# A state-space scan and a two-layer perceptron in one kernel: eleven transfers for a unit's loads instead of twenty, and another order of the head

## The chip, the cores and the metric

One NeuronCore of a Trainium2 chip. The metric is the device time of one execution in microseconds, the median of several runs. The engines are PE (TensorE), DVE (VectorE), ACT (ScalarE), POOL (GpSimd) and SP (SyncE), which here does nothing but issue transfers. [...]

## The reference

Two blocks in a row, all in float32. The first is a Mamba-2 scan (4 sequences, 8 heads, 768 steps, head dimension 32, state dimension 16), given in chunks:

```python
for c in range(nc):
    cum = np.cumsum(log_a[chunk c], axis=-1)
    L = np.exp(cum[i] - cum[j]) * causal
    y_intra = (C @ B.T * L) @ x
    y_inter = (C @ state) * np.exp(cum)
    state = np.exp(sum(log_a)) * state + sum over j of (B[j] x[j] exp(cum[-1] - cum[j]))
```

Its output, as 3072 tokens of 256 features, goes through `h = x @ w_in` (256 to 2048), `g = h * sigmoid(h)` and `g @ w_out` (2048 to 256).

## The kernel before, in words

**Units and pairs.** The 3072 tokens are 12 units of 256 tokens, three to a sequence; a unit has four chunks of Q = 64. The scan of a unit feeds half of the 512 token columns of a pair of units, and the perceptron works pair by pair. Pair 0 (units 0 and 1) uses plain float32 products (`f_s1`, L491, and `f_s2`, L504); pairs 1 to 5 use three products of split numbers (`fp32r`): h, l and d parts of the weights (`WH`, `WL`, `WD`, made by `w_h`, `w_l`, `w_d`, L197 to L209) and of the tokens (`XH`, `XL`, `XD`, made by `f_xh`, `f_xl`, `f_xd`).

**One unit's scan.** DVE's transposes `f_T` (L352), or PE's `f_TP` (L360) for units 1 and 2, give B and C by state. `f_P` scans the decays over each chunk (`pfx`, L311, from `pz`), and `f_C` makes `cw`. `scan_E` (L324) makes the decay matrix E from `ab`, which holds each chunk's decays broadcast over 64 rows, in two halves; `f_B` makes BT from E. Then on PE `f_G` (L402) and `f_D0` (L390), on DVE `f_S` (L422, states) and `f_M` (L408, E times G), on ACT `f_SM`, on PE `f_Y` (L442, L451), and on ACT `f_X`, which copies out the unit's tokens.

**Loads.** `load_unit` (L139) issues everything of a unit on SP's queue: `pz` (4 transfers), B and C by rows (`tbc`, 4 each), B by tokens (`bn`, 2), `ab` (4) and x (2): twenty. Unit 2 has C by tokens in place of the `tbc` loads, so fourteen. `pz` and `ab` come from two DRAM copies of the clipped decays, `a_in` and `a_zero`, which `f_A2` writes in the head. Units 0 and 1 get theirs from the inputs directly.

**Weights.** Sixteen weight pieces of 512 KB arrive as 64-bit numbers (`raw`, six buffers in the pool `quad`); ACT (`w_size`), DVE and POOL (`w_bits`, L181) turn each into float32 (`w32`). `w_bits(n)` then issues the load of piece n + 6, so the place of a `w_bits` in the program also fixes the place of a load in SP's queue. Pieces 0 to 7 are of `w_in`, 8 to 15 of `w_out`.

**Order.** The kernel is under a manual schedule: every engine's order is the order of the calls. The head (L624 to L680) is written out call by call. Then `steps` (L732) lists which `f_s1(u, j)` follows which and what is put between: "2:D b9 s10" is `f_G` and `f_D0` of unit 2, `w_bits(9)`, `w_size(10)`. A second list (L738) does the same around `f_s2(0)` to `f_s2(5)`, written m0 to m5; h, l and d with a number are `w_h`, `w_l`, `w_d`, and `3:h`, `3:l`, `3:d` are `f_xh`, `f_xl`, `f_xd` of unit 3. After that `step(s)` (L755) runs the f32r pairs: `s1_d` (L515) starts a tile's sum and sends it through ACT (L520), `s1_h` (L522) goes on, `s2` and `s2_d` are the second layer. `PLAN` puts the units of the next pair between the steps ("bL" is the load of the second unit after).

**Pools.** `quad` has six buffers of 4 KB a partition, `blk` 76 of 2 KB. `loads` gives `ab`, `tbc` and `bn` one buffer each, `xt` two.

Of the kernel before, what the change touches and what calls it, by code (L numbers as in the profile page):

```python
# [8 lines left out]
FP32 = mybir.dt.float32  # L9
# [24 lines left out]
def kernel(  # L34
# [22 lines left out]
    nc = tc.nc  # L57

    batch, H, S, D = x.shape
    N = B.shape[-1]  # L60
    Q = 64
    UT = 256
# [6 lines left out]

    const = ctx.enter_context(tc.tile_pool(name="const", bufs=1))  # L70
    loads = ctx.enter_context(tc.tile_pool(name="loads", bufs=1))
    quad = ctx.enter_context(tc.tile_pool(name="quad", bufs=6))
    sc = ctx.enter_context(tc.tile_pool(name="sc", bufs=1))
    sc2 = ctx.enter_context(tc.tile_pool(name="sc2", bufs=2))
    blk = ctx.enter_context(tc.tile_pool(name="blk", bufs=1))
    dram = ctx.enter_context(tc.tile_pool(name="dram", bufs=1, space=bass.MemoryType.DRAM))
    ps_s = ctx.enter_context(tc.tile_pool(name="ps_s", bufs=1, space=bass.MemoryType.PSUM))
    ps_h = ctx.enter_context(tc.tile_pool(name="ps_h", bufs=2, space=bass.MemoryType.PSUM))
# [19 lines left out]
    ab, bn, tbc, xt = ({} for _ in range(4))  # L98
# [2 lines left out]
        return u // UPB, u % UPB * UT  # L101

    def load_pa(u, q):
        for c in range(4):
            q.dma_start(out=pz[:, c, 1:], in_=a_in[4 * u + c].rearrange("h (o t) -> h o t", o=1).to_broadcast([H, N, Q]))

    def load_ab(u, q):
        ab[u] = loads.tile([128, 2, H, Q], FP32, name="ab")
        for t in range(4):
            k, c = divmod(t, 2)  # L110
            q.dma_start(out=ab[u][64 * c:64 * c + 64, k], in_=a_zero[4 * u + t:4 * u + t + 1].to_broadcast([64, H, Q]))

    def load_n(u, i, q):
        b, t0 = at(u)
# [8 lines left out]
    def load_t(u, i, q):  # L123
        b, t0 = at(u)
        if u == 0:
            tbc[u] = block("tbc0").rearrange("p (i e r n) -> p i e r n", i=2, e=2, r=8)
        elif u not in tbc:
            tbc[u] = loads.tile([128, 2, 2, 8, N], FP32, name="tbc")
        for g in range(4):
            q.dma_start(out=tbc[u][32 * g:32 * g + 32, i],  # L130
                        in_=(B, C)[i][b, 2 * g:2 * g + 2, t0:t0 + UT].rearrange("e (t r) n -> t e r n", r=8))

    def load_x(u, q):
        b, t0 = at(u)
# [46 lines left out]
    def w_bits(n, parts=1):  # L181
        if n in raw:
            u, v, hi = two(wu.pop(n)), two(wv.pop(n)).bitcast(U32), raw[n][:, :, :, 1]
            nc.vector.tensor_scalar(out=u, in0=u, scalar1=LEAST, scalar2=MOST, op0=ALU.max, op1=ALU.min)
            u = u.bitcast(U32)
            nc.vector.tensor_scalar(out=u, in0=u, scalar1=3, scalar2=None, op0=ALU.logical_shift_left)
            nc.vector.scalar_tensor_tensor(out=v, in0=hi, scalar=0x80000000, in1=v,  # L187
                                           op0=ALU.bitwise_and, op1=ALU.bitwise_or)
            w32[n] = block("w32")
            for i in range(parts):  # L190
                fs = slice(WF // parts * i, WF // parts * (i + 1))
                nc.gpsimd.tensor_tensor(out=two(w32[n])[:, :, fs].bitcast(U32), in0=u[:, :, fs], in1=v[:, :, fs],  # L192
                                        op=ALU.add)
        if n + RAW < NW:
            load_w(n + RAW, nc.sync)
# [13 lines left out]
                                       op0=ALU.mult, op1=ALU.subtract)  # L209


    a_in = dram.tile([batch * S // Q, H, Q], FP32, name="a_in")
    a_zero = dram.tile([batch * S // Q, H, Q], FP32, name="a_zero")
    NC0 = S // Q
    A0, A1 = 96, 96 + NC0
# [30 lines left out]
    def f_A2():  # L246

        r = slice(0, NC0 * batch)
        nc.vector.tensor_scalar(out=acl[r], in0=acl[r], scalar1=1.0, scalar2=1e-6, op0=ALU.min, op1=ALU.max)
        nc.vector.tensor_copy(out=acz[r], in_=acl[r])  # L250
        nc.vector.memset(acz[r, :, 0:1], 0.0)
        nc.sync.dma_start(out=a_in, in_=acl[r])
        nc.sync.dma_start(out=a_zero, in_=acz[r])

    misc = block("misc")
    idle = misc[:, 0:UT].bitcast(BF16)
    nc.vector.memset(idle, 0.0)

    def busy(n, small=0):
        t = half("zero")  # L260
# [55 lines left out]
    def f_P(u):  # L316
        if u < 2:
            f_P0(u)
        f_P1(u)
# [15 lines left out]
    def f_Ek(u, k):  # L335
        scan_E(u, H * k, H, ab.pop((u, k)))
# [8 lines left out]
    def f_B(u, engine=nc.vector):  # L345
        BT[u] = sc.tile([128, 2, H, N], FP32, name="BT")
        engine.tensor_tensor(out=BT[u], in0=bn[u], in1=E[u][:, :, :, Q - 1:Q].to_broadcast([128, 2, H, N]),
                             op=ALU.mult)
# [138 lines left out]
    def f_s1(u, j):  # L487
        hp = two(half("hp"))
        for i in range(2):
            for kc in range(KC):  # L490
                nc.tensor.matmul(out=hp[:, i], lhsT=two(w32[j])[:, kc, 128 * i:128 * i + 128],  # L491
                                 rhs=two(XF[u])[:, kc], start=(kc == 0), stop=(kc == KC - 1))
        GT[u, j] = block("gT")
        nc.scalar.activation(two(GT[u, j]), hp, AF.Silu)
        if j == 7:
            XF.pop(u)
# [17 lines left out]
    def s1_d(s):  # L514
        P, f = 1 + s // NF, s % NF  # L515
        HP[s] = half("hp")
        for kc in range(KC):
            nc.tensor.matmul(out=HP[s], lhsT=two(WD[f // 2])[:, kc, 128 * (f % 2):128 * (f % 2) + 128], rhs=XD[P][:, kc],  # L518
                             start=(kc == 0), stop=False, skip_group_check=True)
        nc.scalar.activation(HP[s], HP[s], AF.Copy, scale=-HALF / UP)  # L520
# [125 lines left out]
    w_size(1)  # L646
    busy(3, 18)
    f_Y(0)
    f_P(1)
    f_Ek(1, 0)  # L650
    f_Ab(1, 1)
    f_X(0)
# [5 lines left out]
        f_T2(1, e)  # L658
    f_s1(0, 1)
    f_Ek(1, 1)  # L660
    f_B(1)
    w_bits(2, 2)
    f_C(1)
# [5 lines left out]
    f_M(1, 0)  # L669
    f_M(1, 1)  # L670
    f_s1(0, 2)
    f_A2()
    load_unit(2)
    w_size(4, "u")
    w_bits(3, 2)
    f_Y(1)
    f_X(1)
    w_size(4, "v")
# [43 lines left out]
    def todo(text):  # L722

        for step in text.split():
            if ":" in step:
                u, what = step.split(":")
                stage(int(u), what)
                continue
            n = int(step[1:].split(".")[0])
            {"b": w_bits, "s": w_size, "h": w_h, "l": w_l, "d": w_d, "m": f_s2, "o": f_out0}[step[0]](n)  # L730

    steps = ((1, 0, ""), (0, 3, "b5 s6"), (1, 1, "b6 s7"), (1, 2, "b7 s8"), (1, 3, "b8"), (0, 4, "2:T"),  # L732
             (1, 4, "2:P"), (0, 5, "2:C12B s9 3:L"), (1, 5, "2:D b9 s10"), (0, 6, "2:SsM"), (1, 6, "b10 s11"),
             (0, 7, "2:Y b11 s12 3:T"), (1, 7, "b12 s13 3:P h0"))
    for u, j, text in steps:
        f_s1(u, j)
        todo(text)
    for text in ("m0 3:C12B 2:h h1 l0 d0 2:l b13 s14", "m1 3:D 2:d 4:L h2 l1 d1 b14 s15", "m2 3:SsM h3 l2 d2 b15",  # L738
                 "m3 3:Y h4 l3 d3", "m4 3:h h5 l4 d4 h8 3:l", "m5 3:d l5 d5 4:T l8 d8"):
        todo(text)  # L740


# [12 lines left out]
    def step(s):  # L755

        last = NF * (NP - 1)
        t = s - LAG
        P, f = 1 + s // NF, s % NF
        ends = t >= 0 and t % NF == NF - 1  # L760
        scans = P + 1 < NP
        if t >= 0:
            PENDING.append(t)
        if s == 0:
            s1_d(0)

        if s < last:
            s1_h(s)
            if s + 1 < last:
                s1_d(s + 1)  # L770
        if scans and f in FIRST:
            stage(2 * P + 2 + "ab".index(FIRST[f][0]), FIRST[f][1:])
        if s == last + 1:
            s2(t)
            s2_d([t, t + 1])
            f_sum2(NP - 1)
            return
        if s == last + 2:
            s2(t)
            f_end(NP - 1)  # L780
            return
        if ends:
            s2_d(PENDING)
            s2(t)
            PENDING.clear()
            f_out(1 + t // NF)
        if s < last:
            s1_g(s)
        if s < 2:
            f_s2(6 + s)  # L790
        if s == 2:
            f_out0(0)
            f_out0(1)
        if t >= 0 and not ends:
            s2(t)
        if PENDING and not (scans and (f < 6 or 9 <= f < 12)):
            s2_d(PENDING)
            PENDING.clear()
        if scans and f == 8:
            f_sum2(P)  # L800
        if 1 <= s <= last:
            s1_gl(s - 1, nc.gpsimd if f in ASIDE and scans else nc.vector)
            s1_gd(s - 1)
        if s >= last:
            return
        if t > 4 and t % NF == 2:
            f_store()
        if scans:
            for what in PLAN.get(f, ()):
                u = 2 * P + 2 + "ab".index(what[0])  # L810
                if f == 15 or what == "aL":
                    u += 2
                if u < NU:
                    stage(u, what[1:])
        if s in PARTS:
            w_h(PARTS[s])
        if s - 1 in PARTS:
            w_l(PARTS[s - 1])
            w_d(PARTS[s - 1])
# [34 lines left out]
```

## Time and profile before

| | before |
|---|---|
| time, median of 3 runs | 349.65 us (349.64 to 349.75) |
| span of the profiled execution | 346.5 us, 7826 instructions |
| PE busy | 324.6 us, 94% |
| DVE busy | 262.6 us, 76% |
| ACT busy | 211.9 us, 61% |
| POOL busy | 66.1 us, 19% |
| DMA | 26.66 MB in 99339 packets |

A busy share is a mean over the whole span. Which engine sets the pace of a stage is seen in the busy times by stretch, in the gaps that an engine's timeline shows, and in the chain of waits, which follows the work that ended last back to what released it. "SPq" is time in which SP issues a transfer. "DMA raw<-..." in a chain is the wait for such a transfer to land.

### The profile page before, as it was taken

The numbers are of one execution on the slowest core, as the hardware profiler recorded it, in microseconds if no ns is written. First come the engines' busy times: TensorE is split into PE (matmuls) and PEld (weight loads), VectorE is DVE, ScalarE is ACT, GpSimd is POOL, SyncE is SP. The second block draws the span as 40 slices with busy tenths as digits, with TensorE's granted clock in tenths as the row PEclk, the third lists the DMA queues.
The fourth block names the chain that finished last, engine by engine and source line by source line (L and its number), as shares of the span: only waits on it lengthen the run. The fifth ranks groups of instructions, "written<-read, shape, count | busy, mean of one in ns | idle before, by whom it ended". The sixth has DMA issues, their size and how long they took to land.

```text
span 346.5 us, 7826 instructions
## 1 busy us (share of the span) xinstructions
PE 324.6 (94%) x3145; PEld 254.3 (73%) x3146; DVE 262.6 (76%) x430; ACT 211.9 (61%) x403; POOL 66.1 (19%) x56
## 2 busy tenths in 40 slices
PE   8977999777998999999999999999999999999991
PEld 4566788666866778777778778778778788788881
DVE  7969975999559998898766896965996853674443
ACT  3656575432467877757775756666676756555651
POOL 3235523120113010242101231202250202000000
PEclk9999999999999999999999999999999999999998
DMA  6975894650171160045340163420153000020003
GB/s 121 209 248 173 168 335 98 145 115 0 48 144 25 38 117 1 18 108 83 67 97 0 34 120 67 88 63 1 48 112 57 2 2 0 0 48 14 0 0 63
DMA packets 99339, 26.66 MB, mean 77 GB/s; under 512 B 87558, under 2 KB 92422, under 8 KB 99302
## 3 DMA queue, kind: packets, MB, share of 16 engines
q1 hardware_dynamic: 95110, 25.76, 33.1%
q10 hardware_dynamic: 4192, 0.39, 0.9%
q8 instruction: 24, 0.39, 0.5%
q14 instruction: 13, 0.11, 0.1%
HBM read 22.80 MB, written 3.34 MB: 75 GB/s over the span
## 4 chain that ended last, share of the span: by engine, by line
PE 70%; DVE 10%; DMA 8%; SPq 8%; issue 2%; ACT 1%; DVEq 0%; ACTq 0%
PE hp L526 22%; PE b L572 11%; PE hp L518 10%; PE oa L559 10%; PE oa L558 10%; DMA raw<-in_moe_w_out_dram 3%; SPq L121 3%; PE oa L504 2%; DVE wl L203 2%; PE gy L451 2%; DMA ab<-a_zero 2%; PE gy L442 1%; DMA a_in<-acl 1%; DMA raw<-in_moe_w_in_dram 1%; PE gy L402 1%
## 5 line engine op out<-in xcount | busy, mean ns | idle before, releaser
L520 ACT ACTIVATE hp<-hp 128x512 f32<-128x512 f32 x80 | 46.6, 582 | 75.0 <-PE hp L518 74.7
L540 DVE TENSOR_TENSOR gl<-g,gh 128x512 fp32r<-128x512 f32 x56 | 38.6, 689 | 47.7 <-ACT gh L536 44.8
L540 POOL TENSOR_TENSOR gl<-g,gh 128x512 fp32r<-128x512 f32 x24 | 39.9, 1663 | 172.4 <-ACT gh L536 156.3
L526 PE MATMUL hp<-xh,wh 128*128 128x512 f32 x160 | 65.6, 410 | 2.6 <-ACT hp L520 2.6
L544 DVE SCALAR_TENSOR_TENSOR gd<-gh,g 128x512 fp32r<-128x512 f32 x80 | 61.9, 776 | 6.0 <-ACT gh L536 6.0
L526 PE MATMUL hp<-xl,wl 128*128 128x512 f32 x160 | 63.2, 395 | 0.0
L559 PE MATMUL oa<-gl,wl 128*128 128x512 f32 x160 | 63.1, 394 | 0.0
L558 PE MATMUL oa<-gh,wh 128*128 128x512 f32 x160 | 62.7, 392 | 0.0
L536 ACT ACTIVATE gh<-g 128x512 fp32r<-128x512 f32 x80 | 50.6, 632 | 2.8
L518 PE MATMUL hp<-xd,wd 128*128 128x512 f32 x160 | 50.4, 396 | 0.0
L534 ACT ACTIVATE g<-hp 128x512 f32<-128x512 f32 x80 | 47.5, 594 | 0.6 <-PE hp L526 0.6
L572 PE MATMUL b<-gd,wd 128*128 128x512 f32 x160 | 44.6, 391 | 0.0
L526 PEld LDWEIGHTS hp<-xh,wh 128*128 128x128 f32 x160 | 30.0, 188 | 13.0 <-ACT hp L520 6.0
L558 PEld LDWEIGHTS oa<-gh,wh 128*128 128x128 f32 x160 | 30.0, 188 | 7.5 <-ACT o L584 0.7
L518 PEld LDWEIGHTS hp<-xd,wd 128*128 128x128 f32 x160 | 30.0, 188 | 7.3
L559 PEld LDWEIGHTS oa<-gl,wl 128*128 128x128 f32 x160 | 30.0, 188 | 7.2
L572 PEld LDWEIGHTS b<-gd,wd 128*128 128x128 f32 x160 | 30.0, 188 | 6.8 <-DVE o L599 0.2
L526 PEld LDWEIGHTS hp<-xl,wl 128*128 128x128 f32 x160 | 30.1, 188 | 5.5
L491 PE MATMUL hp<-xf,w 128*128 128x256 f32 x128 | 30.1, 386 | 4.3 <-POOL w L192 3.0
L192 POOL TENSOR_TENSOR w<-wu,wv 128x512 uint32<-128x512 uint32 (+1 forms) x20 | 23.4, 1178 | 50.5 <-DVE wv L187 47.8
L491 PEld LDWEIGHTS hp<-xf,w 128*128 128x128 f32 x128 | 23.5, 190 | 9.7 <-POOL w L192 4.5
L324 DVE TENSOR_TENSOR_SCAN E<-ab,diag 128x512 f32<-128x512 f32 x24 | 28.7, 1228 | 0.7 <-DMA ab<-a_zero 0.7
(80 smaller groups left out, 367.0 us busy)
## 6 DMA issues: line engine op xcount, KB each, us to landing
ab<-a_zero SPq DMA_DIRECT2D x40, 128.0 KB
raw<-in_moe_w_in_dram SPq DMA_DIRECT2D x8, 512.0 KB
raw<-in_moe_w_out_dram SPq DMA_DIRECT2D x8, 512.0 KB
xt<-in_x_dram SPq DMA_DIRECT2D x24, 128.0 KB
out_dram<-ot SPq DMA_DIRECT2D x44, 64.0 KB
bn<-in_B_dram SPq DMA_DIRECT2D x22, 64.0 KB
tbc<-in_C_dram SPq DMA_DIRECT2D x40, 32.0 KB
pz<-a_in SPq DMA_DIRECT2D x40, 32.0 KB
```

The lines of the kernel that those rows point to most:

```text
L324: nc.vector.tensor_tensor_scan(out=E[u].rearrange("p k h t -> p (k h t)")[:, Q * g0:Q * (g0 + n)], data0=t.rearrange("p g t -> p (g t)"), ...
L491: nc.tensor.matmul(out=hp[:, i], lhsT=two(w32[j])[:, kc, 128 * i:128 * i + 128], rhs=two(XF[u])[:, kc], start=(kc == 0), stop=(kc == KC - 1))
L518: nc.tensor.matmul(out=HP[s], lhsT=two(WD[f // 2])[:, kc, 128 * (f % 2):128 * (f % 2) + 128], rhs=XD[P][:, kc], start=(kc == 0), stop=Fals ...
L520: nc.scalar.activation(HP[s], HP[s], AF.Copy, scale=-HALF / UP)
L526: nc.tensor.matmul(out=HP[s], lhsT=two(w[f // 2])[:, kc, 128 * (f % 2):128 * (f % 2) + 128], rhs=x_[P][:, kc], start=False, stop=(kc == KC ...
L534: nc.scalar.activation(G[s], HP.pop(s), AF.Silu, scale=UP)
L536: nc.scalar.activation(GH[s], G[s], AF.Copy, scale=DOWN)
L540: engine.tensor_tensor(out=GL[s], in0=G[s], in1=GH[s].bitcast(FP32), op=ALU.subtract)
L544: nc.vector.scalar_tensor_tensor(out=GD[s], in0=GH[s].bitcast(FP32), scalar=1.0 + 1.0 / HALF, in1=G.pop(s), op0=ALU.mult, op1=ALU.subtract)
L558: nc.tensor.matmul(out=OA[P][m], lhsT=two(WH[n])[:, r, ms], rhs=gh, start=(f == 0), stop=False)
L559: nc.tensor.matmul(out=OA[P][m], lhsT=two(WL[n])[:, r, ms], rhs=gl, start=False, stop=(f == NF - 1))
L572: nc.tensor.matmul(out=B2[P][:, m], lhsT=two(WD[n])[:, r, 128 * m:128 * m + 128], rhs=gd, start=(fresh and s == tiles[0]), stop=True, skip ...
```

## The change

Each unit's loads become fewer and larger. `pz` comes in one transfer: the DRAM copy `a_in` now lies by heads, with one element of padding ahead of each chunk (rows of Q + 1), so that the four chunks with their leading zeros are one run; a transfer from `misc`, which is zero, writes the padding once. `tbc` comes in two transfers for each of B and C, and `ab` in two, through access patterns written by hand. A unit has eleven transfers for twenty, unit 2 nine for fourteen, and the first load of C in the head two for four.

The rest is order, in the head alone: `f_P(1)` goes behind the second scan of E of unit 1; `w_bits(3)` goes ahead of `f_A2`, and with it the load of weight piece 9 ahead of the writes of `a_in` and of unit 2's loads; unit 3's P, C and E go ahead of `w_bits(12)`, its `f_G` and `f_D0` from behind m1 to behind m0, `f_S`, `f_M` and `f_SM` likewise earlier, `f_Y` from behind m3 to behind m2; the split numbers of units 2 and 3 move with them. `s1_d(0)`, the first product of pair 1, goes from the start of `step(0)` to behind m3 ("p0"). The pool `quad` is opened after `blk` instead of before it, which gives its tiles other addresses.

```diff
-    quad = ctx.enter_context(tc.tile_pool(name="quad", bufs=6))
     sc = ctx.enter_context(tc.tile_pool(name="sc", bufs=1))
     sc2 = ctx.enter_context(tc.tile_pool(name="sc2", bufs=2))
     blk = ctx.enter_context(tc.tile_pool(name="blk", bufs=1))
+    quad = ctx.enter_context(tc.tile_pool(name="quad", bufs=6))
...
     def load_pa(u, q):
-        for c in range(4):
-            q.dma_start(out=pz[:, c, 1:], in_=a_in[4 * u + c].rearrange("h (o t) -> h o t", o=1).to_broadcast([H, N, Q]))
+        q.dma_start(out=pz.rearrange("p c t -> p (c t)"),
+                    in_=a_in[:, 4 * u:4 * u + 4].rearrange("h (o c) t -> h o (c t)", o=1).to_broadcast([H, N, 4 * Q + 4]))
 
     def load_ab(u, q):
         ab[u] = loads.tile([128, 2, H, Q], FP32, name="ab")
-        for t in range(4):
-            k, c = divmod(t, 2)
-            q.dma_start(out=ab[u][64 * c:64 * c + 64, k], in_=a_zero[4 * u + t:4 * u + t + 1].to_broadcast([64, H, Q]))
+        for k in range(2):
+            q.dma_start(out=ab[u][:, k].rearrange("p h t -> p (h t)"),
+                        in_=bass.AP(tensor=a_zero.tensor, offset=a_zero.offset + (4 * u + 2 * k) * H * Q,
+                                    ap=[[H * Q, 2], [0, 64], [1, H * Q]]))
...
-        for g in range(4):
-            q.dma_start(out=tbc[u][32 * g:32 * g + 32, i],
-                        in_=(B, C)[i][b, 2 * g:2 * g + 2, t0:t0 + UT].rearrange("e (t r) n -> t e r n", r=8))
+        src = (B, C)[i]
+        for e in range(2):
+            q.dma_start(out=tbc[u][:, i, e].rearrange("p r n -> p (r n)"),
+                        in_=bass.AP(tensor=src.tensor, offset=src.offset + ((b * H + e) * S + t0) * N,
+                                    ap=[[2 * S * N, 4], [8 * N, 32], [1, 8 * N]]))
...
-    a_in = dram.tile([batch * S // Q, H, Q], FP32, name="a_in")
+    a_in = dram.tile([H, batch * S // Q, Q + 1], FP32, name="a_in")
...
-        nc.sync.dma_start(out=a_in, in_=acl[r])
+        nc.sync.dma_start(out=a_in[:, :, 1:].rearrange("h c t -> c h t"), in_=acl[r])
         nc.sync.dma_start(out=a_zero, in_=acz[r])
 
     misc = block("misc")
     idle = misc[:, 0:UT].bitcast(BF16)
     nc.vector.memset(idle, 0.0)
+    nc.sync.dma_start(out=a_in[:, :, 0:1].rearrange("h c t -> c h t"),
+                      in_=misc[:NC0 * batch, 0:H].rearrange("p (h t) -> p h t", t=1))
...
-    f_P(1)
     f_Ek(1, 0)
...
     f_Ek(1, 1)
+    f_P(1)
...
     f_s1(0, 2)
+    w_bits(3, 2)
     f_A2()
     load_unit(2)
     w_size(4, "u")
-    w_bits(3, 2)
...
-             (0, 7, "2:Y b11 s12 3:T"), (1, 7, "b12 s13 3:P h0"))
+             (0, 7, "2:Y b11 s12 3:T"), (1, 7, "3:PC12B b12 s13 h0"))
...
-    for text in ("m0 3:C12B 2:h h1 l0 d0 2:l b13 s14", "m1 3:D 2:d 4:L h2 l1 d1 b14 s15", "m2 3:SsM h3 l2 d2 b15",
-                 "m3 3:Y h4 l3 d3", "m4 3:h h5 l4 d4 h8 3:l", "m5 3:d l5 d5 4:T l8 d8"):
+    for text in ("m0 3:D 4:L 3:SsM 2:h h1 2:l 2:d l0 d0 b13 s14", "m1 h2 l1 d1 b14 s15", "m2 3:Y 3:h l2 d2 3:l 3:d b15 h3",
+                 "m3 l3 d3 h4 p0", "m4 h8 l4 d4 h5 l8 d8", "m5 4:T l5 d5"):
...
-        if s == 0:
-            s1_d(0)
-
```

More of the change, by code (lines that the diff above doesn't have):

```diff
@@ L729, in todo @@
             n = int(step[1:].split(".")[0])
-            {"b": w_bits, "s": w_size, "h": w_h, "l": w_l, "d": w_d, "m": f_s2, "o": f_out0}[step[0]](n)
+            {"b": w_bits, "s": w_size, "h": w_h, "l": w_l, "d": w_d, "m": f_s2, "p": s1_d}[step[0]](n)
     steps = ((1, 0, ""), (0, 3, "b5 s6"), (1, 1, "b6 s7"), (1, 2, "b7 s8"), (1, 3, "b8"), (0, 4, "2:T"),
              (1, 4, "2:P"), (0, 5, "2:C12B s9 3:L"), (1, 5, "2:D b9 s10"), (0, 6, "2:SsM"), (1, 6, "b10 s11"),
-             (0, 7, "2:Y b11 s12 3:T"), (1, 7, "b12 s13 3:P h0"))
+             (0, 7, "2:Y b11 s12 3:T"), (1, 7, "3:PC12B b12 s13 h0"))
     for u, j, text in steps:
```

## The prediction

> **What bounds the kernel now.** I read the busy shares by stretch first, because the page's 94% for TensorE is a mean over unlike stages. Columns: stretch, its length, then busy time (with instruction count) of PE, weight load, DVE, ACT, POOL, then clock, DMA share, GB/s.
>
> ```profile
> 50.00:60.00 10.00, 10.00 (x137) 8.56 (x136) 4.99 (x10) 6.24 (x13) 3.49 (x3) 1.00 0.52 130
> 60.00:70.00 10.00, 7.94 (x97) 6.53 (x96) 9.23 (x13) 4.74 (x9) 2.30 (x2) 1.00 0.59 144
> 70.00:80.00 10.00, 7.71 (x118) 6.50 (x117) 9.82 (x19) 3.89 (x9) 2.86 (x2) 1.00 0.48 95
> 140.00:180.00 40.00, 40.00 (x462) 31.18 (x461) 33.78 (x55) 27.60 (x54) 8.99 (x6) 1.00 0.41 81
> ```
>
> From 110 us to the end PE has no gap: the head decides. Next, PE's timeline in the head (start, length, work, and in brackets the gap ahead and who ended it):
>
> ```profile
> 64.51 0.46 PE L390 MATMUL gy<-xt,BT 64*32 64x64 f32 x32 [2.06 <-DVE BT L347]
> 74.36 0.58 PE L442 MATMUL gy<-cw,sm 32*64 32x64 f32 x24 [2.29 <-DVE E L408]
> 85.24 0.50 PE L526 MATMUL hp<-xh,wh 128*128 128x512 f32 x1 [1.94 <-ACT hp L520]
> ```
>
> With the smaller gaps of 17 to 43 us (1.03, 0.17, 0.55, 0.47, 1.85, 0.25, 0.50) these make 11.1 us of PE idle before the first f32r product at 85.24; I call that moment T0. All after T0 is a fixed PE schedule, so the new time is 349.65 plus the shift of T0. What set the gaps is in the chain of waits (start, length, link):
>
> ```profile
> 26.52 4.87 DMA a_in<-acl
> 31.41 0.65 SPq L105
> 37.11 2.45 DMA ab<-a_zero
> 43.47 9.93 DMA raw<-in_moe_w_out_dram
> 59.12 3.56 DMA ab<-a_zero
> 62.77 1.23 DVE E L324
> ```
>
> The chain is the load queue: `a_in` to DRAM, unit 2's loads, six weight loads, unit 3's loads, then the scan E of unit 3. [...] So unit 3's issues wait for weight landings; the queue's own waits show it:
>
> ```profile
> SPq L130 <- DMA raw<-in_moe_w_out_dram: 3.8, 4, 1.4
> ```
>
> The last view is the packet count of the DMA section, and the peak of DMA rate in one microsecond:
>
> ```profile
> DMA packets 99339, 26.66 MB, mean 77 GB/s; under 512 B 87558, under 2 KB 92422, under 8 KB 99302
> 49.00:50.00 1.00, 1.00 (x6) 0.87 (x6) 0.92 (x2) 0.99 (x4) 0.01 (x1) 1.00 1.05 404
> ```
>
> [...] Data pieces under 512 B, from the shapes: 28 loads of B or C by rows x 1024, 24 of x x 1024, 48 stores x 512, 40 of pz x 128, 5 of `a` x 96, one mark: 83,425. The page has 87,558, so 4,133 completions. Take k = 8 for pz and pa01 (their source begins with 8 heads), 12 for `ach` and `acl`, 1 for the mark and 16 for the other 234: 3744 + 328 + 60 + 1 = 4,133. With 16 engines for pz and pa01 it would be 328 more. [...] the trace's best microsecond, 404 GB/s over 16, gives 25.3 GB/s, and I use that. [...]
>
> **The change, part by part.**
>
> *Fewer transfers.* Unit 3's twenty issues become eleven. At the 0.46 to 0.63 us of one issue (four of pz 2.53, four of tbc 1.82, four of ab 2.52) that is nine issues, about 5 us, off SP for unit 3. In the head's stalled stretch it would be worth most of the 2.06, 2.29 and 1.94 us.
>
> But the shapes change k. pz stays at 8. tbc's source now begins with 4, so k = 4. `load_ab`'s source now begins with 2 (`[[H*Q, 2], [0, 64], [1, H*Q]]`), so k = 2, where it was 64 rows on 16 engines. One new ab transfer is 262 KB: 131 KB for each of two engines, 131/25.3 = 5.2 us; the unit's two go to the same two engines, 10.4 us. Bounds: [...] 5.9 us at the mean of 43 to 51 us (355 GB/s). These two engines also carry a sixteenth of all else, in order: 1.3 us for each weight load (32.8 KB).
>
> *`a_in` in padded rows.* 384 pieces of 256 B and 384 zeros of 4 B for 48 pieces of 2 KB. One issue more (0.4 us)[...].
>
> *w_bits(3) ahead of f_A2.* It fills 2.57 us in which DVE waited for acl (23.5 to 26.1), so PE loses its 1.85 us wait. But its weight load 9 now goes ahead of `a_in`: 524 KB at 355 GB/s, 1.5 us. So unit 2's pz issue moves from 31.41 to about 33.
>
> *f_P(1) later, order of 3:C12B, D, M, Y and xl/xd, s1_d(0) ahead of m4.* The same instructions on the same engines. f_P(1)'s move gives PE 0.5 to 1 us near 18 to 23. s1_d(0) (0.5 us) gets its ACT step hidden under two f_s2 of 3.45 us, so the 1.94 us gap goes. D of unit 3 now stands after m0 instead of m1, so m1 is queued behind its wait. *Pool order*: addresses only, no instruction; nothing.
>
> **The sum.** Early PE gains of about 2 us end at unit 2's transposes (before: 38.19), whose loads land no earlier. pz 33.0, tbc and bn to 35.9, ab issued by 37.1[...].
> - ab of unit 2 lands at 43.0 and 48.2 (before: E's two scans at 41.3 and 43). On DVE, E's second scan waits with BT, w_bits(9), S and M queued behind it; on SP, unit 3's pz waits for the same landing[...] with all of unit 3 behind it. BT ends at 49.8, so f_D0(2) starts at 49.9 for 45.78: PE waits 5 us.
> - PE then: three f_s1 (5.4), f_Y (1.5), f_s1(1,7) (1.8), m0 (3.45): 62.5, then it waits for unit 3.
> - The two engines after 47.6: x 1.6, weight loads 10 to 14 6.5, pz, tbc and bn of unit 3 about 5 (tbc 4 x 16 KB an engine[...]; bn 0.7 each), ab of unit 3 10.4: 71.1, landed 71.7. [...]
> - E, BT end at 73.4; f_D0(3) ends at 73.8. Before it ended at 64.97, with m1 already done.
> - Then PE has m1, m2, f_Y, m3: 85.7. XD of unit 3 needs DVE: w_bits(12), S, M to 77.0, then ten operations of 0.6, two w_bits of 1.5 and one stall beside POOL of 1.1 (as at L203, 1.75 for 0.68): 87.1. s1_d(0), m4, m5: 94.5.
> - [...]
>
> T0 moves from 85.24 to 95.2: +10.0, **359.7 us**. [...] Later units hide it: ab of unit 7 is issued from 150.9 and its scan starts at 167.7; 12 us of transfer and landing end near 163.
>
> **Rivals.**
> 1. *ab keeps 16 engines* (the row of broadcasts is split otherwise). Then weight 14 lands by 49, unit 3's ab by 52, before f_D0(3) needs it at 57. PE runs from 25 us with about 1.5 us of waiting at the transposes; T0 near 77, **341.3 us**. For it: the 11.1 us of gaps, and the new order suits early loads. Against: the count of completions.
> 2. *Two engines each, but the two transfers on different pairs.* Half the backlog: unit 2's ab by 43.4, no PE wait; unit 3's by 63, T0 near 85: **349.2 us**. [...]
> 3. *Later units stall as well*: with stores (0.6 us an issue)[...] the 4.7 us of slack of odd units is used up, five times 1 us or so: **365 us**. For it: unit 7's slack. Against: PE's order is fixed, and DVE has idle time.
>
> **How the numbers follow.** Forecast 0.72, rival 1 0.14, rival 2 0.05, rival 3 0.09. Slower than 350.35: forecast, rival 3 and a part of rival 2, 0.83; faster 0.14; within 0.2% 0.03. The range: forecast[...], 356 to 364; rival 3 to 366; and down to 353[...].
>
> **What would show it.** In the profile after: ab's wait at L324 in the tens of microseconds of the head, PE idle of some 5 us ahead of f_D0 of unit 2 and some 11 us of unit 3; DMA share near 2/16 with about 50 GB/s while PE waits; packets under 512 B lower by the pz pieces (4 to 1 a unit) and completions as 2 for each ab. It is wrong if E of unit 3 starts by 55 us (rival 1), or if PE has gaps after 110 us (rival 3).

## The result, and the profile after

The kernel after takes **361.31 us** (median of 4 runs, 361.06 to 362.23); the kernel before 349.70 us (four runs, 349.64 to 351.29). The ratio is 1.033, with a 95% interval of 1.029 to 1.036: slower by 11.6 us. The profiled executions have spans of 360.5 and 346.5 us, 14.0 us apart; each of the two lies about 0.9 us off its kernel's median, in opposite directions, so the traces show some 2 us more than the times.

Busy times by stretch, kernel after (length; PE, weight load, DVE, ACT, POOL with counts; granted clock, DMA share, GB/s):

```profile
50.00:60.00 10.00, 6.02 (x68) 4.62 (x63) 6.32 (x13) 2.85 (x6) 1.92 (x2) 0.68 0.76 250
60.00:70.00 10.00, 10.00 (x142) 8.26 (x148) 3.66 (x7) 7.21 (x15) 1.90 (x2) 0.98 0.44 109
70.00:80.00 10.00, 0.58 (x32) 0.34 (x32) 2.93 (x4) 0.00 (x0) 0.00 (x0) 0.70 0.37 95
140.00:180.00 40.00, 40.00 (x404) 31.77 (x404) 36.60 (x59) 28.50 (x55) 8.69 (x6) 1.00 0.23 55
```

From 70 to 80 us PE is busy for 0.58 us and ACT and POOL not at all. Two microseconds of that stretch, in the same view:

```profile
72.00:74.00 2.00, 0.00 (x0) 0.00 (x0) 0.97 (x1) 0.00 (x0) 0.00 (x0) 1.00 0.12 44
```

A DMA share of 0.12 is 2 engines of 16: everybody waits for two of them, at 44 GB/s. From 140 us on PE is full, as before. The clock column (the third number from the end) is new: 0.68 and 0.70 in the two stretches in which PE waited, 1.00 in the same stretches before.

PE's timeline in the head, kernel after (start, length, work, in brackets the gap ahead and who ended it):

```profile
41.25 0.92 PE L365 MATMUL tp<-ident,bn 128*128 128x128 f32 x2 [4.54 <-DMA bn<-in_B_dram]
54.52 0.65 PE L395 MATMUL gy<-xt,BT 64*32 64x64 f32 x24 [3.98 <-DVE BT L352]
80.00 0.68 PE L395 MATMUL gy<-xt,BT 64*32 64x64 f32 x32 [9.42 <-DVE BT L352]
101.93 0.58 PE L531 MATMUL hp<-xh,wh 128*128 128x512 f32 x1
```

These are the transposes of unit 2, `f_D0` of unit 2, `f_D0` of unit 3, and T0. T0 is the first product of `s1_h(0)`; the first f32r products of all are those of `s1_d(0)`, ahead of it in both kernels (82.48 before, 94.65 after). The 1.94 us gap ahead of T0 is gone, as the early `s1_d(0)` was to achieve, but T0 itself went from 85.24 to 101.93. DVE's scans of E, kernel after:

```profile
47.53 1.23 DVE L329 TENSOR_TENSOR_SCAN E<-ab,diag 128x512 f32<-128x512 f32 x1 [3.26 <-DMA ab<-a_zero]
52.78 1.22 DVE L329 TENSOR_TENSOR_SCAN E<-ab,diag 128x512 f32<-128x512 f32 x1 [4.03 <-DMA ab<-a_zero]
73.03 1.23 DVE L329 TENSOR_TENSOR_SCAN E<-ab,diag 128x512 f32<-128x512 f32 x1 [5.13 <-DMA ab<-a_zero]
78.26 1.22 DVE L329 TENSOR_TENSOR_SCAN E<-ab,diag 128x512 f32<-128x512 f32 x1 [4.01 <-DMA ab<-a_zero]
```

The two halves of a unit's `ab` arrive 5.25 and 5.23 us apart, in both units: that is the time of one 262 KB transfer, 50 GB/s. The chain of waits, kernel after, has the same two transfers as its long links:

```profile
28.76 7.64 DMA a_in<-acl
36.46 0.62 SPq L104
...
40.51 12.24 DMA ab<-a_zero
52.78 1.24 DVE E L329
...
65.95 12.29 DMA ab<-a_zero
78.26 1.24 DVE E L329
```

These 12.24 and 12.29 us stand against 2.45 and 3.56 us for `ab` before. The first line of the chain is a second loss: `a_in` takes 7.64 us from its issue, where it took 4.87. What the first does to the load queue behind it is seen in SP's timeline, first before, then after (start, length of the issues together, what they load, how many):

```profile
39.07 1.16 SPq L137 DMA_DIRECT2D xt<-in_x_dram  x2
40.33 3.56 SPq L170 DMA_DIRECT2D raw<-in_moe_w_out_dram  x6
```

```profile
41.06 8.26 SPq L140 DMA_DIRECT2D xt<-in_x_dram  x2
49.42 5.20 SPq L173 DMA_DIRECT2D raw<-in_moe_w_out_dram  x5
```

Behind the two transfers of `ab` the issue of two small loads of x takes 8.26 us instead of 1.16, and the weight loads behind them are issued some 9 us later than before (3.6 of these were there when `ab` was issued). e3 below, where only `ab` is changed, has the same (8.03 us); e1 and e2, where the patterns of `ab` begin with 64, do not (1.16 and 1.22).

Packets, from the page's DMA section, kernel after:

```profile
DMA packets 94330, 26.67 MB, mean 74 GB/s; under 512 B 81318, under 2 KB 87462, under 8 KB 94294
```

Of the pieces counted for before, the 5,120 of `pz` are now of 1,040 B and leave the count, and 768 of `a_in` (384 of 256 B, 384 of 4 B) come in: 79,073 pieces of data, which leaves 2,245 of the 81,318 packets.

The trace also records the time of each completion. As it lands, a transfer of `ab` has two of them here and had 16 before; one of `tbc` has 4 (16 before), one of `pz` 8 in both kernels, one of x or of a weight piece 16 (the loads of x behind `ab` 14 and then 2). With k the number of a transfer's completions, 2 for the 20 transfers of `ab`, 4 for the 38 of `tbc`, 8 for the ten of `pz` and the one of `pa01`, 16 for 119 others (one of them the zeros), 12 for five and 1 for the mark, the sum is 40 + 152 + 88 + 1,904 + 60 + 1 = 2,245, all of the packets that are left.

The two transfers of `ab` of unit 2 have their completions at 47.40 and 47.51 and at 52.64 and 52.76 us. The first load of x behind them has 14 completions from 45.8 to 46.3 us and its last two at 53.1 and 53.2. In unit 3 it is the same: 72.78 and 72.94, 78.09 and 78.24, and the first load of x with 14 completions by 71.6 and two at 78.5 and 78.7. I read this as both transfers on the same two engines, one behind the other, with the later load's share on these two behind both.

### The profile page after: what moved, and what is told of

It reads as the page before. It is cut to its first block, busy times and chain, and to the rows that moved or that the text cites. A ratio compares the mean times of both kernels' runs of the same rounds, so it can differ in the third digit from the quotient of the medians.

```text
span 360.5 us, 7712 instructions
## 1 busy us (share of the span) xinstructions
PE 329.0 (91%) x3146; PEld 260.0 (72%) x3146; DVE 261.8 (73%) x430; ACT 212.1 (59%) x403; POOL 63.3 (18%) x56
## 2 busy tenths in 40 slices
DMA packets 94330, 26.67 MB, mean 74 GB/s; under 512 B 81318, under 2 KB 87462, under 8 KB 94294
## 4 chain that ended last, share of the span: by engine, by line
PE 70%; DMA 11%; DVE 8%; SPq 7%; ACT 1%; issue 1%; ACTq 0%
PE hp L531 20%; PE b L577 10%; PE hp L523 10%; PE oa L563 10%; PE oa L564 10%; DMA ab<-a_zero 7%; PE oa L509 4%; SPq L122 3%; DMA raw<-in_moe_w_in_dram 2%; DMA a_in<-acl 2%; PE gy L456 2%; PE hp L496 2%; PE gy L447 1%; DVE wd L211 1%; PE gy L407 1%; SPq L173 1%
## 5 line engine op out<-in xcount | busy, mean ns | idle before, releaser
L545 POOL TENSOR_TENSOR gl<-g,gh 128x512 fp32r<-128x512 f32 x24 | 38.1, 1587 | 169.9 <-ACT gh L541 135.0
L523 PE MATMUL hp<-xd,wd 128*128 128x512 f32 x160 | 49.5, 390 | 0.1
L496 PE MATMUL hp<-xf,w 128*128 128x256 f32 x128 | 34.1, 428 | 1.6 <-DVE st L427 1.1
L195 POOL TENSOR_TENSOR w<-wu,wv 128x512 uint32<-128x512 uint32 (+1 forms) x20 | 22.4, 1127 | 70.8 <-DVE wv L190 67.5
L496 PEld LDWEIGHTS hp<-xf,w 128*128 128x128 f32 x128 | 27.2, 217 | 7.2 <-POOL w L195 1.8
```

The costliest lines, as they stand in the source:

```text
L545: engine.tensor_tensor(out=GL[s], in0=G[s], in1=GH[s].bitcast(FP32), op=ALU.subtract)
```

## The experiments

e1, e2, e5 to e7, e9 and e10 are the kernel after with one edit or more; e3, e4, e8, e11 and e12 are the kernel before with a part of the change or one edit. Ratios are against the kernel before in the same set of runs; its median was 348.86 to 350.28 us from set to set, so times of different sets can differ by 1.4 us for that reason alone. T0 and the spacing of products come from one trace of each kernel.

### The shape of `ab`, undone and alone

Undone, e1: four transfers of 64 rows, everything else as after.

```diff
-        for k in range(2):
-            q.dma_start(out=ab[u][:, k].rearrange("p h t -> p (h t)"),
-                        in_=bass.AP(tensor=a_zero.tensor, offset=a_zero.offset + (4 * u + 2 * k) * H * Q,
-                                    ap=[[H * Q, 2], [0, 64], [1, H * Q]]))
+        for t in range(4):
+            k, c = divmod(t, 2)
+            q.dma_start(out=ab[u][64 * c:64 * c + 64, k], in_=a_zero[4 * u + t:4 * u + t + 1].to_broadcast([64, H, Q]))
```

> The changed kernel with load_ab of before: four transfers of 64 rows, everything else as changed. Theory (the two engines of ab set the head): the two scans of E of unit 2 and of unit 3 no longer stand 5.25 us apart, DVE's 16.4 us of waits on ab at L324 go below 3 us, the waits of PE ahead of f_D0 of unit 2 (3.98 us) and unit 3 (9.42 us) go, the first f32r product comes near 84 us instead of 101.93, and the time is near 345 us. Rival (the later a_in, weight piece 9 ahead of it and tbc on four engines set the head, ab is only behind them): the waits move elsewhere and the time stays above 355 us.

Measured: 345.11 us (343.54 to 346.82), ratio 0.989 (0.984 to 0.993); T0 at 86.5. The theory's time came, and the two long waits of PE went; T0 is 2.5 us later than its 84, with waits of 2.66 us left at unit 2's transposes, 1.40 ahead of `f_D0` of unit 3 and 2.13 ahead of `s1_d(0)`.

In two transfers still, but cut by rows instead of by halves, e2: same number of transfers, same bytes, and about the same issue time on SP (1.31 us for unit 2's two, 1.07 in the kernel after).

```diff
-        for k in range(2):
-            q.dma_start(out=ab[u][:, k].rearrange("p h t -> p (h t)"),
-                        in_=bass.AP(tensor=a_zero.tensor, offset=a_zero.offset + (4 * u + 2 * k) * H * Q,
-                                    ap=[[H * Q, 2], [0, 64], [1, H * Q]]))
+        for c in range(2):
+            q.dma_start(out=ab[u][64 * c:64 * c + 64].rearrange("p k h t -> p k (h t)"),
+                        in_=bass.AP(tensor=a_zero.tensor, offset=a_zero.offset + (4 * u + c) * H * Q,
+                                    ap=[[0, 64], [2 * H * Q, 2], [1, H * Q]]))
```

> The changed kernel with ab still in two transfers a unit, but cut the other way: 64 partitions and both halves in each, so that source and destination both begin with a count of 64. Theory (the count of the slowest dimension sets the number of engines): as with four transfers, E's scans close together, near 344 us (two issues of some 0.5 us fewer than with four). Rival (a broadcast source in few large transfers is slow whatever its cut, or the number of transfers sets it): the scans of E stay 5 us apart and the time stays near 361 us.

Measured: 346.29 us (344.84 to 348.66), ratio 0.992 (0.989 to 0.994); T0 at 86.0. DVE's scans of E of units 2 and 3 in e2:

```profile
44.07 2.34 DVE L329 TENSOR_TENSOR_SCAN E<-ab,diag 128x512 f32<-128x512 f32 x2 [1.24 <-DMA ab<-a_zero]
61.10 2.34 DVE L329 TENSOR_TENSOR_SCAN E<-ab,diag 128x512 f32<-128x512 f32 x2 [2.42 <-DMA ab<-a_zero]
```

Both halves run in one group: the 5.25 us between them are gone. Two transfers with 64 as the slowest count cost nothing that can be told from four; two with 2 as the slowest count cost some 15 us. So it is neither the number of transfers, nor their size, nor the broadcast. T0 is at 86.5 and 86.0 in e1 and e2 and was at 85.24 before: even with the long waits for `ab` gone the other fewer transfers and the new order do not bring T0 forward.

Alone, e3: the kernel before with only the new `load_ab`.

```diff
-        for t in range(4):
-            k, c = divmod(t, 2)
-            q.dma_start(out=ab[u][64 * c:64 * c + 64, k], in_=a_zero[4 * u + t:4 * u + t + 1].to_broadcast([64, H, Q]))
+        for k in range(2):
+            q.dma_start(out=ab[u][:, k].rearrange("p h t -> p (h t)"),
+                        in_=bass.AP(tensor=a_zero.tensor, offset=a_zero.offset + (4 * u + 2 * k) * H * Q,
+                                    ap=[[H * Q, 2], [0, 64], [1, H * Q]]))
```

> The kernel before with only load_ab of the change. Theory: ab alone loses more than the whole change; E's halves 5.2 us apart for units 2 and 3, f_D0 of unit 2 about 4 us later and of unit 3 about 11 us later, 358 to 361 us. Rival (the order of the head is what loses): below 352 us.

Measured: 363.78 us (363.46 to 364.46), ratio 1.042 (1.039 to 1.046); T0 at 100.04. PE's gaps ahead of `f_D0` of units 2 and 3 in e3:

```profile
51.35 0.65 PE L391 MATMUL gy<-xt,BT 64*32 64x64 f32 x24 [5.25 <-DVE BT L348]
79.32 0.68 PE L391 MATMUL gy<-xt,BT 64*32 64x64 f32 x32 [9.52 <-DVE BT L348]
```

This one edit costs 14.8 us, more than the whole change and above the theory's 358 to 361 us. The rest of the change gives some 3 us back, nearly all of it through the pool's place (e4).

### The order and the pool

e4, the kernel before with only the pool of 4 KB tiles opened behind that of 2 KB tiles:

```diff
-    quad = ctx.enter_context(tc.tile_pool(name="quad", bufs=6))
     sc = ctx.enter_context(tc.tile_pool(name="sc", bufs=1))
     sc2 = ctx.enter_context(tc.tile_pool(name="sc2", bufs=2))
     blk = ctx.enter_context(tc.tile_pool(name="blk", bufs=1))
+    quad = ctx.enter_context(tc.tile_pool(name="quad", bufs=6))
```

> The kernel before with only the pool of 4 KB tiles opened behind that of 2 KB tiles. Theory A (the addresses set the pace of the f32r products, which after their start took 258.6 us in the changed kernel and 261.3 us before): 346.5 to 347.5 us, with about 2.72 us for a step of twelve products instead of 2.78. Theory B (the pace differs for another reason, and an address costs nothing, as forecast): 349.7 us.

Measured: 346.31 us (344.84 to 348.96), ratio 0.993 (0.990 to 0.995). T0 is unchanged (85.31). The twelve products of a plain step take 2.72 us where they took 2.78. So the pool's place, which changes addresses only, is worth some 2.6 us. (From T0 to the end this one trace is only 1.0 us shorter than that of before: 1.6 us went to the clock just behind T0, as the last section shows.)

e8, the kernel before with the new order of the head and the pool's new place, all loads as before (the pool as in e4, and of the order these edits among the others):

```diff
+    w_bits(3, 2)
     f_A2()
     load_unit(2)
     w_size(4, "u")
-    w_bits(3, 2)
...
-    for text in ("m0 3:C12B 2:h h1 l0 d0 2:l b13 s14", "m1 3:D 2:d 4:L h2 l1 d1 b14 s15", "m2 3:SsM h3 l2 d2 b15",
+    for text in ("m0 3:D 4:L 3:SsM 2:h h1 2:l 2:d l0 d0 b13 s14", "m1 h2 l1 d1 b14 s15", "m2 3:Y 3:h l2 d2 3:l 3:d b15 h3",
```

> The kernel before with only the new order of the head and the new place of the pool: every load as before, twenty transfers a unit. Theory (the order is worth a little, the pool's place 2.7 us): T0 stays within 1 us of 85.3, time 345 to 347, the same as the pool's place alone (346.3). Rival A (the new order needs the fewer transfers, since it wants unit 3 sooner): T0 at 87 or later, time 348 to 350. Rival B (the order is good by itself and the new loads of tbc and pz take it away): T0 at 83.5 or sooner, time 342 to 344.

Measured: 347.69 us (345.69 to 349.43), ratio 0.993 (0.991 to 0.996), T0 at 86.27. The ratio is e4's and T0 lies just inside the theory's 1 us; the time alone stands between the theory and rival A, but the kernel before was 1.1 us slower in this set of runs than in e4's. So the new order by itself brings nothing that was measured. It takes away the gap ahead of T0, but `f_D0` of unit 3 now stands ahead of m1, and PE waits 4.39 us for it there.

### The other loads

e5 (on e1): `w_bits(3)` back behind `load_unit(2)`, so that the load of weight piece 9 is behind unit 2's loads.

```diff
-    w_bits(3, 2)
     f_A2()
     load_unit(2)
     w_size(4, "u")
+    w_bits(3, 2)
```

> The kernel after with ab in four transfers of 64 rows (345.1 us, first f32r product T0 at 86.5), and with w_bits(3) moved back behind load_unit(2), so that the load of weight piece 9 no longer stands ahead of the writes of a_in. Theory (the late a_in sets what is left): pz of unit 2 is issued near 31.5 instead of 35.2, the 2.66 us gap ahead of unit 2's transposes shrinks to under 1 us, T0 moves to about 83.5, time about 342. Rival (DVE's order is worth more: w_bits(3) behind f_A2 brings back DVE's 2.57 us wait and PE's 1.85 us wait): T0 stays at 86 to 87, time 345 to 346.

Measured: 345.92 us (344.92 to 347.08), ratio 0.990 (0.986 to 0.994), T0 at 86.69: the rival's numbers. `pz` of unit 2 was issued at 34.98, not near the theory's 31.5. From the issue of `a_in` to that of unit 2's `pz` it is 6.8 us, with 8.05 in e1. The gap at unit 2's transposes fell from 2.66 to 0.34 us, and the gap ahead of `f_D0` of unit 3 rose from 1.40 to 3.19.

e6 (on e1): `tbc` in the four transfers of before.

```diff
-        for e in range(2):
-            q.dma_start(out=tbc[u][:, i, e].rearrange("p r n -> p (r n)"),
-                        in_=bass.AP(tensor=src.tensor, offset=src.offset + ((b * H + e) * S + t0) * N,
-                                    ap=[[2 * S * N, 4], [8 * N, 32], [1, 8 * N]]))
+        for g in range(4):
+            q.dma_start(out=tbc[u][32 * g:32 * g + 32, i],
+                        in_=(B, C)[i][b, 2 * g:2 * g + 2, t0:t0 + UT].rearrange("e (t r) n -> t e r n", r=8))
```

> The kernel after with ab in four transfers (345.1 us), and tbc too in the four transfers of before (16 engines instead of 4). Theory (tbc on four engines is the same fault as ab on two, only smaller): the load of tbc in the first 16 us ends about 1.2 us sooner, a_zero and a_in are written 1 to 2 us sooner, E of unit 3 waits 0 instead of 1.14 us, T0 moves from 86.5 to about 84.5, time about 343. Rival (64 KB is too little to matter on four engines, and four more issues cost SP about 2 us for unit 3): time 345 to 347.

Measured: 345.44 us (343.67 to 347.69, and one at 349.68), ratio 0.987 (0.985 to 0.989), T0 at 84.28. T0 agrees with the theory, the time with the rival (345 to 347, where the theory had 343); the ratio is lower than e1's by 0.001, inside both intervals. `tbc` in two transfers may cost a little; the times don't show it.

e7 (on e1): `a_in` in dense rows without the transfer of zeros, `pz` in four transfers.

```diff
-    a_in = dram.tile([H, batch * S // Q, Q + 1], FP32, name="a_in")
+    a_in = dram.tile([batch * S // Q, H, Q], FP32, name="a_in")
...
+        for c in range(4):
+            q.dma_start(out=pz[:, c, 1:], in_=a_in[4 * u + c].rearrange("h (o t) -> h o t", o=1).to_broadcast([H, N, Q]))
```

> The kernel after with ab in four transfers (345.1 us), and with a_in in dense rows as before, without the transfer of zeros, and pz in four transfers. Theory (the padded a_in lands late because of 384 pieces of 256 B and 384 of 4 B): the wait for a_in falls from about 7.6 to about 6.5 us, pz of unit 2 is issued about 1.4 us sooner, but three more issues of 0.63 us give it back for unit 2: time 344.5 to 345.5. Rival (one pz transfer for four is what pays): pz's issues hold unit 2's and unit 3's loads back by 2 us each, time 346.5 to 348.

Measured: 345.69 us (345.26 to 346.19), ratio 0.990 (0.986 to 0.994), T0 at 85.2. From the issue of `a_in` to that of `pz` 5.4 us instead of 8.05: beside e1 the padding costs 2.7 us there, more than the theory's 1.1. In the time nothing is seen of it.

e9 (on e6): the padding made in SBUF, so that `a_in` is written in one transfer with pieces of 260 B and no 4 B pieces (`acp` is a tile with rows of Q + 1, into which the decays are loaded and clipped; to make room for it the pool of 2 KB tiles has 75 buffers instead of 76).

```diff
-        nc.sync.dma_start(out=a_in[:, :, 1:].rearrange("h c t -> c h t"), in_=acl[r])
+        nc.sync.dma_start(out=a_in.rearrange("h c t -> c h t"), in_=acp[r])
```

> The kernel after with ab and tbc in four transfers each (345.4 us, T0 84.28, a_in waited for 7.0 us), and with the padding of a_in made in SBUF: the clipped decays lie in a tile with rows of 65, so a_in is written in one transfer of 260 B pieces and the 384 zeros of 4 B fall away. Theory A (the pieces of a_in are mis-sized, but unit 3's loads decide T0): the wait for a_in falls to about 5.5 us and pz of unit 2 is issued 1.5 us sooner, but the gap that goes at unit 2's transposes (2.5 us) comes back ahead of f_D0 of unit 3 (3.5 us, then about 5): T0 within 0.7 of 84.3, time 344.5 to 346. Theory B (the late a_in decides): T0 at 82.5, time 343 to 344.

Measured: 345.93 us (343.93 to 347.60), ratio 0.991 (0.988 to 0.994), T0 at 84.46, 6.2 us from `a_in` to `pz` for 7.0 in e6. T0 and the time are theory A's, its path is not shown: 0.8 us was gained where 1.5 had been expected, and neither gap moved by more than 0.2 us (2.34 for 2.54 at unit 2's transposes, 3.38 for 3.47 ahead of `f_D0` of unit 3), so that nothing came back at the second that had gone at the first.

e10 (on e9): weight pieces 13 and 14 loaded behind unit 3's loads.

```diff
-        if n + RAW < NW:
+        if n + RAW < NW and n not in (7, 8):
...
-"2:C12B s9 3:L"
+"2:C12B s9 3:L w13 w14"
```

"w" followed by a number is a weight piece's load.

> The run before this one (ab and tbc in four transfers, padding in SBUF) with the loads of weight pieces 13 and 14 issued behind unit 3's loads instead of ahead of them. Theory (weight pieces ahead in the queue are what holds unit 3 back, whatever the shape of its own loads): the loads of B and C no longer wait for weight landings (3.6 us), E of unit 3 starts by 56 us instead of 59 to 61, the gap ahead of f_D0 of unit 3 is under 1 us, T0 80.5 to 82, time 341 to 342.5. Rival (the bytes have to pass anyway, and pieces 13 and 14 now land late): w_bits(13) and w_bits(14) wait on DVE, PE waits ahead of m5 or of the first f32r product, T0 84 or later, time 345 or more.

Measured: 344.35 us (343.98 to 344.78), ratio 0.987 (0.985 to 0.990), T0 at 83.69. It is the lowest time of all kernels here, though the interval of its ratio overlaps e9's, and e6 has the same ratio. SP's waits for weight pieces from 40 to 56 us, first in e9, then in e10 (us in total, times, longest):

```profile
SPq L130 <- DMA raw<-in_moe_w_out_dram: 4.6, 4, 1.9
```

```profile
SPq L130 <- DMA raw<-in_moe_w_out_dram: 1.8, 1, 1.8
```

The theory's mechanism is there: the gap ahead of `f_D0` of unit 3 went from 3.38 us to none. Its size was missed, in time (341 to 342.5 expected) and in T0: E of unit 3 starts at 58.44, not by 56, and T0 moved by 0.8 and not by 3, while in this trace the gap at unit 2's transposes was 4.34 us (2.34 in e9), where DVE had waited 4.24 us for the decays to land (1.41 in e9).

### The spacing of the f32r products

e11, the kernel before with the 4 KB pool opened between the small pools and the 2 KB pool, so that the 2 KB tiles keep their addresses:

```diff
-    quad = ctx.enter_context(tc.tile_pool(name="quad", bufs=6))
     sc = ctx.enter_context(tc.tile_pool(name="sc", bufs=1))
     sc2 = ctx.enter_context(tc.tile_pool(name="sc2", bufs=2))
+    quad = ctx.enter_context(tc.tile_pool(name="quad", bufs=6))
     blk = ctx.enter_context(tc.tile_pool(name="blk", bufs=1))
```

> The kernel before with the pool of 4 KB tiles opened just ahead of the pool of 2 KB tiles: the 2 KB tiles keep the addresses that they have in the kernel before, and only the 4 KB tiles move (by the size of two small pools). Theory A (the place of the 2 KB tiles, which hold the weights' parts, sets the spacing of the f32r products): the spacing of twelve stays at 2.78 us, time 349 to 350. Theory B (the place of the 4 KB tiles, which hold the tokens' parts, sets it): 2.72 us, time 346 to 347.

Measured: 346.83 us (345.13 to 347.99), ratio 0.993 (0.991 to 0.996); 2.72 us for twelve.

e12, the kernel before with the small pools behind the 2 KB pool, so that the 4 KB tiles keep their addresses:

```diff
     quad = ctx.enter_context(tc.tile_pool(name="quad", bufs=6))
-    sc = ctx.enter_context(tc.tile_pool(name="sc", bufs=1))
-    sc2 = ctx.enter_context(tc.tile_pool(name="sc2", bufs=2))
     blk = ctx.enter_context(tc.tile_pool(name="blk", bufs=1))
+    sc = ctx.enter_context(tc.tile_pool(name="sc", bufs=1))
+    sc2 = ctx.enter_context(tc.tile_pool(name="sc2", bufs=2))
```

> The kernel before with the two small pools of the scan (15 KB) opened behind the pool of 2 KB tiles: the 4 KB tiles keep their place of the kernel before, the 2 KB tiles move down by 15 KB, the small tiles move to the end. Theory A (the place of the 4 KB tiles, right behind the loads, sets the spacing of the f32r products): twelve of them take 2.78 us as in the kernel before, time 348.5 to 350. Theory B (another place is the cause, that of the small pools or of the 2 KB tiles): 2.72 us, time 346 to 347.

Measured: 347.72 us (346.02 to 349.89), ratio 0.994 (0.991 to 0.997); 2.72 us for twelve.

e11 speaks for the place of the 4 KB tiles, and e12 against it. Nor are the operands' own addresses enough: in e11 the second layer's products, whose operands are all 2 KB tiles, have sped up too (0.231 to 0.227 us from one to the next, in 290 to 330 us) without having moved. All three other arrangements of these pools give 2.72 us, and only that of the kernel before gives 2.78. What in it does so stays open.

## Why the prediction was right

The forecast case came: slower, through `ab` on two engines, with all of the loss in the head. By its steps:

| step | forecast | trace after |
|---|---|---|
| `pz` of unit 2 issued | 33.0 | 36.46 |
| one `ab` transfer on its two engines | 5.2 us | 5.25 us |
| E of unit 2, second half | 48.2 | 52.78 |
| unit 2's transposes on PE | as before (38.19) | 41.25 |
| PE's wait ahead of `f_D0` of unit 2 | 5 us | 3.98 us |
| E of unit 3, second half | 71.7 | 78.26 |
| PE's wait ahead of `f_D0` of unit 3 | 11 us | 9.42 us |
| T0 | 95.2 | 101.93 |
| from T0 to the end | as before | 2.7 us shorter |

**The mechanism.** That a pattern which begins with 2 runs on two engines was the author's assumption. What the trace of before shows of it is the number of completions, 8 for `pz` with its 8 heads and 16 for `ab` with its 64 rows; of a pattern that begins with 2 it shows nothing. The runs agree: 5.25 us a transfer at 50 GB/s, a DMA share of 0.12, the two completions of each transfer, e1 and e3 (the edit undone and alone, 0.989 and 1.042), and e2 (0.992), where only the order of the cut differs. One link of the path was not the forecast's: there, unit 3's `pz` was to wait for the landing of unit 2's `ab`. SP's waits from 20 to 75 us in the kernel after have none for `ab`; the queue was held already where it issued the loads of x, 8.26 us for the two. Why an issue takes so long behind transfers on two engines is not shown.

**The step that failed: the landing times, hence T0's shift of 10.0.** It measured 16.7. The error of 6.7 is there when unit 3's `ab` lands (6.6 late against the forecast), and does not grow after. It has three parts.

1. *`a_in`.* Unit 2's `pz` was issued 3.5 us later than forecast. The padding's small pieces had been put at 0.4 us, the author's estimate, which the trace of before does not show. From the issue of `a_in` to that of `pz` it is 7.0 to 8.05 us with the padding in two transfers (after, e1, e2, e6), and 5.4 and 4.8 without (e7, e8): 2 to 3 us. Piece 9 had been put at 1.5; e5 beside e1 gives 1.3, e8 none (4.8 us, with 4.87 before), and e9 and e10, alike up to there, differ by 1.1 (6.2 and 5.1), so no run shows it clearly. `a_in` itself was issued at 28.76 instead of 26.52, where no shift was forecast. In the five traces with `tbc` in two transfers (after, e1, e2, e5, e7) it was issued at 27.1 to 28.8; with four it was at 26.6 in e6 and e9, but at 27.9 in e8 and 29.2 in e10, so its parts stay unseparated. By the time `ab` was issued, 2.85 of the 3.5 was left (39.95 for 37.1).
2. *`ab` of unit 2.* From its issue to the first scan it took 7.6 us for 5.9, a further 1.7. A fixed part looks to be left out: from the end of its issue to its last completion the first transfer took 7.0 us in unit 2 and again in unit 3, 1.8 more than the 5.25 that the second one adds, and before, one of 128 KB with 16 completions took 2.1 to 2.7.
3. *The weight loads.* From unit 2's second half to unit 3's it took 25.5 us for 23.5. The completions say which term was too small. The last of x is at 53.8, the last of weight load 14 at 62.8: 9.0 us for the weights, where the forecast had 6.5. What follows fits: 4.8 us until `ab` begins, reckoned back from its completions (forecast about 5), and 10.6 for `ab` (10.4). The completions of the four `tbc` in these 4.8 us come 0.8 to 1.3 us apart, for 64 KB with 4 completions each. The forecast had the weight loads waiting on the two engines already; they were issued only from 49.42 to 54.62.

**A second error, which hid part of the first.** The pool's order had been put at nothing, since it changes addresses only. That failed. It is worth 2.7 us after T0 in the trace, and a ratio of 0.993 in e4. So 359.7 came as near 361.31 as it did partly by luck: a shift 6.7 too small and a gain of 2.7 left out, with the 2 us by which these two traces overstate the difference.

**The clock.** The forecast's 95.2 is 94.5 and 0.7 us for a slower PE behind the last gap, the author's estimate: the trace of before shows no slowed PE (clock 1.00). PE's busy time up to T0 (the second number of each line), before and after:

```profile
0.00:85.24 85.24, 72.44 (x916) 55.42 (x917) 72.21 (x132) 44.77 (x89) 26.20 (x32) 1.00 0.65 164
```

```profile
0.00:101.93 101.93, 79.61 (x916) 60.94 (x917) 70.60 (x130) 44.28 (x88) 25.19 (x32) 0.88 0.54 137
```

Of T0's 16.7 us, 9.5 are more idle time, and 7.2 are an equal number of products (916) taking longer. The granted clock was 0.50 from 39.96 to 46.79, from 53.61 to 60.44 and from 74.09 to 84.33 us; each stretch begins inside one of the gaps of 4.54, 3.98 and 9.42 us and goes on behind it. There 24 products of `f_s1` took 7.52 and then 8.07 us where 24 had taken 5.45, and the two `f_s2` behind `f_D0` of unit 3 took 8.99 for 7.17. The forecast had named only the third. It did not spoil T0, as far as the trace shows: the first two slow stretches are followed by waits for `ab`, which a faster PE would only have lengthened, and after the third PE came to `s1_d(0)` at 94.55, when DVE had just made the last of XD (94.6). From the end of `f_D0` of unit 3 to T0 the forecast had 21.4 us and the trace has 21.3.

**The rivals.** Rival 1 (16 engines, T0 near 77, 341.3 us) did not come, and e1 and e2 show that its number was wrong too: with `ab` cut by 64 T0 is at 86 there. It let unit 3's `ab` land by 52, where it is waited for until 59.8 in e1. Part of what holds it is the queue: in e9 the loads of B and C wait 4.6 us for weight pieces, and with two pieces moved behind (e10) 1.8. The rest of the way from 86 to 77 stays open; T0 gained 0.8 us in e10. Rival 2 (different pairs of engines) falls with the 5.25 us between halves and with the completions of x. Rival 3 (later units stall) falls: after T0 PE has two gaps, 0.67 and 1.41 us, where the kernel before has 0.67 and 1.35, and none from 125 us on.

## What to carry to other kernels

When a load is rewritten as one access pattern, look at the count of its outermost dimension before the count of transfers: here a pattern that started with 2 took 5.25 us for 262 KB, at 50 GB/s and with 2 completions where there had been 16, and the same bytes cut the other way, with 64 outermost, cost nothing that was measured (346.29 us, with 345.11 for four transfers). Count what stands behind such a transfer as well: two small loads took 8.26 us to issue instead of 1.16, and all weight loads came later. Price a small transfer that others wait for by its pieces (the padded `a_in` cost 2 to 3 us), and expect a gain at one wait to come back at the next, as in e5, while a load queue that waits for earlier landings (4.6 us in e9) decides. And an edit that changes only addresses is not free of effect until it has been timed by itself (0.993 in e4).

## What the runs showed that had not been expected

The place of the pools in SBUF changes the spacing of matrix products that stand on an engine without gaps, by 2% (2.78 to 2.72 us for twelve, the same in the one trace of every kernel with the same arrangement), with the cause open.

The granted clock fell in short gaps. In the kernel after the gaps of 4.54, 3.98 and 9.42 us went with stretches at 0.50 of 6.83, 6.83 and 10.24 us. In e4 and in e11 it fell with a gap of 1.96 and 1.97 us ahead of T0; in the kernel before, with a gap of 1.94 at the same place, it stayed at 1.00. Busy times by stretch, e4, just after that gap (PE's clock is the third number from the end):

```profile
86.00:88.00 2.00, 2.00 (x6) 1.53 (x5) 0.08 (x1) 0.18 (x1) 0.00 (x0) 0.50 0.14 32
```

From T0 to the second step it then took 6.39 us instead of 4.77, so 1.6 us went with it. It is not a matter of a few hundredths. The 32 products of `f_s2` behind `f_D0` of unit 3 took 8.86 us after a gap of 1.99 us in e4, 8.82 after 2.03 in e11 and 8.43 after 2.49 in e12, but 7.17 after 2.06 us in the kernel before. A gap of 2.29 us there left the clock at 1.00, and after 2.58 us in e8 the products of `f_s1` from 20 to 60 us took 384 ns on average, with 385 before. So in this range the length does not decide, and what does stays open. The stretch at half clock behind T0 lasted 3.4 us in e4 and in e11, by the clock of the windows of 2 us.
